# Up products listed ahead of the activation of their bank's other half, and the last quarters listed anew

## The chip, the cores and the metric

The kernel runs on one core of a Trainium2 chip. The metric is device time in microseconds, of the one core. Five engines work side by side, each through its own instruction list in order: TensorE (PE in the profile; its weight loads are PEld), VectorE (DVE), ScalarE (ACT), GpSimd (POOL) and SyncE (SP), which here issues DMAs. An instruction waits, through semaphores, for those of other engines that it depends on.

## The reference

Eight batches of eight heads go through an attention over 32 memory slots; the result, 4608 tokens by 512, goes through two dense layers with a leaky activation between them.

```python
a = softmax(phi over the 32 slots)
k_m, v_m = einsum('bhsm,bhsd->bhmd', a, k), einsum('bhsm,bhsd->bhmd', a, v)
attn = softmax(q @ k_m.T / sqrt(64))
x = attn @ v_m                      # as 4608 x 512
h = x @ w_in                        # 512 x 2048
out = maximum(0.01 * h, h) @ w_out  # 2048 x 512
```

## The kernel before

The value slots of a batch are folded into the first weight matrix (steps `W`), so the up product takes the attention weights themselves. Numbers are split in a high and a low float16 half, and every product is made of three: high by high, high by low, low by high. The order of all work is written out by hand as two strings of step names, `OPENING` and `LATER` (line 67); `run` (line 1447) calls the steps one after the other inside `manual_schedule` (line 1452). Each engine gets its own instructions in that order. Dependencies are drawn from the same order: an instruction waits for the earlier listed ones on other engines that touch what it touches.

The names that matter, with their lines:

- From token 1152 on, the tokens go in groups `G` of 256, each in four quarters `k` of the hidden width (56 quarters; the last group, quarters 52 to 55, has 128 tokens).
- `p{k}.{i}` (`up_late`, line 1215; matmuls at 1229): the up product of part `i` (0 to 3) of quarter `k`. All of them write one PSUM bank, `banks["ph"]`: even `i` its half 0, odd `i` its half 1. A group that spans two batches has two sets of six matmuls.
- `v{k}.{i}` (`leaky_late`, 1245): the activation on ScalarE, out of that half, into the float32 buffer of the quarter. There are two such buffers, taken in turn.
- `s{k}` (`add_g`, 1266, VectorE): sums and differences for a product scheme with seven products in place of eight. `c{k}.{h}` (1270, ScalarE) casts the high half of operand group `h` (0 or 1), `l{k}.{h}` (1274, VectorE) makes the low half.
- `d{k}.{n}` (`down_late`, 1297; `down_tile`, 1331, in the last group): the seven (or four) down products of the quarter. `x{G}.…` (1307 to 1317) combines a group's sums, `z{G}.{t}` (`finish`, 1321) scales one output tile on ScalarE and sends it from SyncE in four DMAs. `end` (`store`, 1170 and 1171) evacuates and sends the last tile; it writes the buffer that `z15.1` sent from.
- `a{b}.…` are the attention's steps of batch `b`: `B20` (664) the exponential, `C10` (698) the slot products on PE, `C3k` (736) scales the key slots on ScalarE, `D10` (772) transposes them on PE, `D11` (785) the value slots, `D2` (344) a small spreading product, `q0` and `q1` (575) eight loads of q each, `Q0` and `Q1` (836) flip q on VectorE, `E1` and `E3` (861) are the scores, `S01` to `S08` the second softmax. `W{b}{j}.p` (1020) folds, `.h` and `.l` split the folded weights.

Of the kernel before, what the change touches and what calls it, by code (L numbers as in the profile page):

```python
# [74 lines left out]
O11.0 o1.m3 P14.0 o2.l1 V14.0 C13 o2.s0 P14.1 L13 o2.m0 O11.1 a2.B10 V14.1 o1.n3 o2.n0 o2.s1 P15.0
a2.B20 C14 o2.m1 O12.0 o2.s2 V15.0 o2.n1 o2.m2 a2.C10 L14 P15.1 o2.s3 a2.B3 O12.1 o2.l2 a2.q0 V15.1
o2.n2 o3.s0 a2.q1 o3.k1 o3.k0 o3.l1 P16.0 P16.1 o3.k2 O13.0 V16.0 C15 o2.m3 o3.s1 O13.1 V16.1 C16
o3.l0 o3.s2 o3.m1 a2.C2 a2.C30 i0.l1 o3.l2 o3.m2 P17.0 L15 o3.m3 o3.n3 O14.0 V17.0 L16 a3.phi P17.1
a2.Q0 a2.C3k V17.1 C17 O14.1 o3.n1 a2.D10 i0.l0 a2.Q1 a2.D3 P18.0 O15.0 V18.0 a2.C31 o3.n2 i0.l2
O15.1 o3.m0 P18.1 a2.E1 a2.E22 a2.E3 a3.kv3 i1.k0 L17 a2.E21 a2.E23 V18.1 i1.l0 P19.0 a2.E20 a2.C4  # L80
i1.k1 Z1.2 a3.kv2 P19.1 a2.D11 a2.S01 C18 Z1.1 a3.kv1 Z1.0 a2.S02 L18 V19.0 O16.0 i1.k2 a2.D2 a2.D4
a3.kv0 a2.S03 i1.l2 O16.1 a2.D5 a2.D6 a2.S04 V19.1 P20.0 C19 O17.0 O17.1 o2.n3 V20.0 L19 P20.1
V20.1 i1.l1 C20 i2.k0 P21.0 W20.p a2.S05 i2.k1 O18.0 W20.h0 V21.0 W20.h1 i2.k2 P21.1 L20 O18.1
W20.l1 V21.1 W20.l0 C21 i2.l0 W21.p a2.S06 P22.0 W21.h1 W21.h0 i2.l1 O19.0 V22.0 o3.n0 i2.l2 W21.l0
i3.k1 P22.1 O19.1 i3.k0 W22.p V22.1 a3.A1 i3.k2 L21 a3.A2 W22.h0 P23.0 W22.h1 O20.0 V23.0 a2.S07
P23.1 a3.A4 O20.1 V23.1 a2.S08 i3.l2 C22 i3.l0 W22.l1 C23 W21.l1 O21.0 i3.l1 L23 p0.0 W23.p v0.0
p0.1 W23.h0 p0.2 L22 a3.A3 W23.h1 a3.B10 O21.1 W22.l0 v0.1 a3.B20 W23.l1 a3.C10 O22.0 os2 a3.B3
v0.2 a3.q0 W23.l0 a4.phi a3.C2 p0.3 a3.C30 a3.q1 O22.1 v0.3 a3.C3k s0 c0.0 a3.C31 l0.0 c0.1 a3.D10
l0.1 p1.0 p1.1 a3.D11 v1.0 O23.0 v1.1 a3.C4 p1.2 a3.D3 v1.2 p1.3 a3.Q0 O23.1 v1.3 p2.0 Z2.0 Z2.1 s1
d0.0 Z2.2 p2.1 v2.0 d0.1 v2.1 a3.D2 a4.A1 a3.D4 c1.0 d0.2 c1.1 p2.2 l1.0 d0.3 v2.2 a3.D5 d0.4 a4.A2  # L90
p2.3 a4.A4 p3.0 a3.Q1 a3.D6 l1.1 d0.5 v2.3 a3.E1 a3.E22 d0.6 a3.E3 c2.0 s2 c2.1 p3.1 a3.E23 v3.0
d1.0 v3.1 a3.E20 d1.1 a3.E21 W30.p l2.0 a3.S01 os3 d1.2 a4.kv3 W30.h0 p3.2 W30.h1 a4.kv1 d1.3 v3.2
a4.kv0 d1.4 W30.l0 d1.5 l2.1 W30.l1 p3.3 a3.S02 W31.p a4.kv2 v3.3 c3.0 d1.6 W31.h0 s3 W31.h1 p4.0
a3.S03 p4.1 v4.0 d2.0 v4.1 c3.1 d2.1 a4.A3 l3.0 d2.2 p4.2 d2.3 v4.2 a3.S04 d2.4 d2.5 a4.B10 a3.S05
p4.3 W31.l1 v4.3 p5.0 l3.1 a3.S06 v5.0 d2.6 a4.B20 d3.0 a3.S07 p5.1 W31.l0 a4.C10 s4 v5.1 a3.S08
d3.1 x3.p a4.q0 c4.0 a4.B3 p5.2 d3.2 c4.1 d3.3 x3.0 v5.2 d3.4 p5.3 l4.0 v5.3 x3.1 c5.0 l4.1 x3.2 s5
d3.5 d3.6 p6.0 x3.3 p6.1 l5.0 v6.0 d4.0 p6.2 a4.q1 v6.1 c5.1 d4.1 d4.2 z3.1 a5.phi d4.3 p6.3 l5.1
v6.2 v6.3 d4.4 a4.C2 a4.C30 d4.5 d4.6 p7.0 p7.1 a4.Q0 d5.0 a4.C3k s6 a4.D10 c6.0 a4.D3 l6.0 v7.0
# [12 lines left out]
p14.1 v14.0 d12.0 a5.q1 p14.2 a5.B3 d12.1 d12.2 l13.1 a5.C2 a5.C30 d12.3 a5.Q0 v14.1 v14.2 d12.4
a6.phi a5.C3k p14.3 d12.5 v14.3 a5.D10 a5.D3 c14.0 d12.6 s14 p15.0 a5.C31 v15.0 l14.0 c14.1 p15.1
d13.0 a5.Q1 l14.1 v15.1 d13.1 z5.1 d13.2 p15.2 d13.3 v15.2 d13.4 d13.5 d13.6 p15.3 p16.0 a5.E1
a5.E22 a5.C4 a5.E3 a6.kv2 a5.E23 a5.E20 d14.0 v15.3 z5.0 c15.0 s15 p16.1 a6.kv3 a5.D11 v16.0 a6.kv0
v16.1 a5.D2 a5.D4 c15.1 d14.1 d14.2 a5.D5 a6.kv1 l15.1 p16.2 d14.3 v16.2 a5.E21 d14.4 p16.3 l15.0
d14.5 v16.3 W42.p c16.0 a6.A1 s16 d14.6 W42.h1 p17.0 W42.h0 W42.l1 a5.S01 a5.D6 p17.1 v17.0 W42.l0
# [12 lines left out]
d22.6 c24.0 p25.0 W52.l1 a6.A3 W52.l0 p25.1 v25.0 a6.B10 l24.0 d23.0 v25.1 d23.1 x8.p c24.1 d23.2
x8.0 p25.2 l24.1 d23.3 v25.2 d23.4 x8.1 p25.3 x8.2 a6.B20 d23.5 v25.3 W53.p c25.0 s25 d23.6 W53.h0  # L130
p26.0 W53.h1 p26.1 x8.3 v26.0 d24.0 W53.l1 z8.1 a6.C10 v26.1 c25.1 a6.q0 d24.1 W53.l0 l25.0 d24.2
p26.2 l25.1 p26.3 v26.2 d24.3 d24.4 d24.5 v26.3 c26.0 s26 c26.1 d24.6 a6.B3 p27.0 p27.1 v27.0 d25.0
p27.2 v27.1 l26.1 a6.q1 a6.C2 d25.1 a6.C30 l26.0 d25.2 a6.C31 p27.3 d25.3 a7.phi v27.2 a6.C3k a6.C4
a6.D10 v27.3 s27 a6.D11 d25.4 a6.Q0 z8.0 d25.5 a6.D3 c27.0 d25.6 c27.1 p28.0 a6.D2 a6.D4 p28.1
v28.0 d26.0 v28.1 a6.D5 l27.1 d26.1 a6.Q1 d26.2 p28.2 d26.3 a6.D6 v28.2 a7.A1 p28.3 p29.0 a6.E1
a6.E22 d26.4 a6.E3 a7.kv3 a6.E20 a6.E23 d26.5 v28.3 a6.E21 W60.p l27.0 c28.0 s28 a7.kv2 d26.6
W60.h0 W60.l0 l28.0 p29.1 a7.kv0 v29.0 a6.S01 d27.0 v29.1 d27.1 x9.p os6 c28.1 d27.2 a7.kv1 W61.p
W60.h1 x9.0 p29.2 l28.1 W61.h0 d27.3 v29.2 W61.h1 d27.4 x9.1 p29.3 x9.2 d27.5 a6.S02 v29.3 d27.6
c29.0 p30.0 x9.3 p30.1 s29 v30.0 d28.0 v30.1 d28.1 l29.0 c29.1 d28.2 p30.2 l29.1 d28.3 v30.2 z9.1
# [1345 lines left out]
```

## Time and profile before

| what | us |
|---|---|
| time, median of 3 runs | 653.35 |
| lowest, highest | 652.09, 653.45 |
| the profiled execution, from first to last instruction | 653.44 |
| ScalarE's up activations of the late part (line 1245), 224 | 99.3 busy, 466 ns each |
| down products of the late part (line 1297), 2184 matmuls | about 287 busy in three groups |
| the last group's down products (1331) | 1% of the chain |

In the profile the engines' busy times stand first, then the chain of work that ended last, followed back from the end: what it names is what the time was spent on. A list of waits says, for each line of an engine, which line of another engine ended its idle time: total, count, longest. In a timeline each row has start, duration, engine, line, operation, operands, count and, in brackets, the idle time before it with what ended it. Rows of like instructions that follow each other are merged into one.

### The profile page before, as it was taken

Reading aid. Unit: us, or ns where it says so; the run is one execution under the profiler, and the core shown is the slowest. Engines: PE = TensorE matmul, PEld = TensorE weight load, DVE = VectorE, ACT = ScalarE, POOL = GpSimd, SP = SyncE. Lnnn points to the kernel's source line nnn. Section 1 sums busy time; section 2 is a strip of 40 time slices with the busy share of each in tenths; the row PEclk is TensorE's granted clock in tenths of the full one; section 3 lists DMA queues with packets and bytes.
Section 4 is the critical chain, followed back from the end, with each engine's and each line's share of the span. In section 5 each row is a group of like instructions: output and inputs, shape, how many; then the busy total and the mean of one; then the engine's idle time right before and its main releaser. Section 6 shows DMA issues by size and latency. Waiting matters only on the chain.

```text
span 653.4 us, 17090 instructions
## 1 busy us (share of the span) xinstructions
PE 635.2 (97%) x7256; PEld 476.3 (73%) x7256; DVE 515.4 (79%) x863; ACT 392.5 (60%) x671; POOL 29.5 (5%) x37
## 2 busy tenths in 40 slices
...
DVE  5675889998996899899969975889887897575641
...
GB/s 237 405 340 332 246 89 85 46 7 104 194 3 25 142 155 56 111 124 35 25 117 158 1 33 43 11 134 146 34 15 80 27 29 22 14 29 6 34 1 50
DMA packets 85309, 61.16 MB, mean 94 GB/s; under 512 B 61936, under 2 KB 68336, under 8 KB 85232
## 3 DMA queue, kind: packets, MB, share of 16 engines
q1 hardware_dynamic: 85136, 59.94, 33.3%
q8 instruction: 57, 0.93, 0.6%
...
## 4 chain that ended last, share of the span: by engine, by line
PE 94%; DMA 2%; ACT 2%; SPq 1%; DVE 0%; issue 0%; ACTq 0%
PE po L1297 31%; PE ph L1229 22%; PE po L1186 16%; PE ph L1114 8%; PE ph L1297 5%; PE pa L1020 4%; PE pa L698 3%; DMA arena<-in_moe_w_in_dram 2%; PE po L1331 1%; PE pa L861 1%; PE pa L1387 1%; ACT wi L1245 1%; PE pa L887 0%; PE pa L344 0%; SPq L549 0%
## 5 line engine op out<-in xcount | busy, mean ns | idle before, releaser
L1297 PEld LDWEIGHTS <-arena 128*128 128x128 f16 x2184 | 209.9, 98 | 31.9 <-issue 8.8
L1245 ACT ACTIVATE wi<-ph,g_sc 128x256 f32<-128x256 f32 (+1 forms) x224 | 99.3, 466 | 164.4 <-PE ph L1229 156.9
L1229 PE MATMUL ph<-a,w_mem 128*128 128x256 f16 (+3 forms) x1440 | 145.3, 246 | 2.9 <-ACT wi L1245 2.9
L1229 PEld LDWEIGHTS <-w_mem 128*128 128x128 f16 x1440 | 114.6, 98 | 17.9 <-issue 6.3
L1297 PE MATMUL po<-arena 128*128 128x256 f16 x936 | 122.2, 273 | 0.0
L1297 PE MATMUL po<-wo,arena 128*128 128x256 f16 x936 | 122.1, 273 | 0.0
L1186 PE MATMUL po<-wo,arena 128*128 128x512 f16 (+1 forms) x384 | 110.3, 433 | 0.0
L1274 DVE TENSOR_TENSOR arena<-arena 128x1024 f16<-128x1024 f32 x52 | 63.6, 1223 | 22.4 <-ACT arena L1270 22.4
L1274 DVE TENSOR_TENSOR arena<-wi,arena 128x768 f16<-128x768 f32 (+1 forms) x60 | 54.7, 912 | 10.1 <-ACT arena L1270 10.1
L1266 DVE TENSOR_TENSOR arena<-wi 128x256 f32<-128x256 f32 x104 | 40.4, 430 | 25.6 <-ACT wi L1245 25.1
L1270 ACT CAST arena<-arena 128x1024 f16<-128x1024 f32 x52 | 54.5, 1047 | 8.2 <-DVE arena L1266 8.0
L1114 PE MATMUL ph<-a,w_mem 128*128 128x192 f16 (+2 forms) x304 | 52.2, 317 | 0.7 <-ACT t L936 0.7
L1186 PEld LDWEIGHTS <-arena 128*128 128x128 f16 x288 | 27.9, 98 | 29.7 <-issue 0.6
L1270 ACT CAST arena<-wi 128x768 f16<-128x768 f32 (+1 forms) x60 | 46.6, 777 | 1.5
L1266 DVE TENSOR_TENSOR arena<-wi,arena 128x256 f32<-128x256 f32 x104 | 45.8, 440 | 1.8
L1297 PE MATMUL ph<-wo,arena 128*128 128x256 f16 x312 | 42.6, 273 | 0.0
L985 POOL TENSOR_TENSOR a<-t,a 128x1024 f16<-128x1024 f32 (+2 forms) x16 | 21.9, 1385 | 431.9 <-ACT a L980 431.9
L1186 PEld LDWEIGHTS po<-wo,arena 128*128 128x128 f32 x96 | 17.7, 190 | 20.3 <-issue 18.5
L1020 PE MATMUL pa<-wi,vT 64*32 64x512 f16 (+1 forms) x704 | 28.9, 420 | 0.4 <-ACT vT L805 0.4
L1114 PEld LDWEIGHTS <-w_mem 128*128 128x128 f16 x240 | 20.7, 98 | 10.3 <-issue 4.1
L1053 ACT ACTIVATE w_mem<-pa 128x512 f16<-128x512 f32 x40 | 22.7, 596 | 8.4 <-PE pa L1020 7.4
L1121 ACT ACTIVATE arena<-ph,g_sc 128x384 f32<-128x384 f32 x32 | 18.4, 581 | 15.6 <-PE ph L1114 15.3
...
## 6 DMA issues: line engine op xcount, KB each, us to landing
out_dram<-obs SPq DMA_DIRECT2D x142, 64.0 KB, 1.7
...
```

The lines of the kernel that those rows point to most:

```text
L698: nc.tensor.matmul(var["pk"][g][hh * M:(hh + 1) * M, cs], ld["phi"][rows, hh, j, :], ld["kv", hh][rows, kinds[0]:kinds[-1] + 1, j, :], sta ...
L985: nc.gpsimd.tensor_tensor(piece(lo, tb), piece(t2, tb), piece(hi, tb), ALU.subtract)
L1020: nc.tensor.matmul(pf[g][cols, :], lhs, rhs, start=(n == 0), stop=(n == len(passes) - 1), tile_position=(g * D, hh * M),)
L1053: nc.scalar.activation(tiles(halves(w16(b, j), g)[:, 0]), w(g), AF.Copy, scale=ws)
L1114: nc.tensor.matmul(ph[:, t0:t0 + n * SB], lhs, rhs, start=(m == 0), stop=(m == len(seq) - 1))
L1186: nc.tensor.matmul(po, lhs, rhs, start=(f == 0 and m == 0), stop=(f == NQ * NF - 1 and m == len(seq) - 1),)
L1229: nc.tensor.matmul(ph[:, t0:t0 + n], lhs, rhs, start=(m == 0), stop=(m == len(seq) - 1))
L1245: nc.scalar.activation(dst, ph, AF.Prelu, scale=g_sc2[:, j:j + 1], alpha=SLOPE)
L1266: nc.vector.tensor_tensor(gt[:, x], y, z, op)
L1270: nc.scalar.copy(dst[:, 0], src)
L1274: nc.vector.tensor_tensor(dst[:, 1], src, dst[:, 0], ALU.subtract)
L1297: nc.tensor.matmul(acc, g[:, x, s, u], rhs, start=(h == 0 and j == 0 and u == 0 and m == 0), stop=(j == NQ - 1 and u == 1 and m == 2), ski ...
```

## The change

Only the string `LATER` changes. It has the same 1834 steps; some thirty stand at another place. No step is added, removed or altered. The string is wrapped at a fixed width, so the diff rewrites many lines; below are its moves, with the neighbours of each, by letters that are used from here on.

```diff
 A
-p1.2 a3.D3 v1.2 p1.3 a3.Q0 O23.1 v1.3 p2.0
+p1.2 p1.3 a3.D3 v1.2 a3.Q0 O23.1 v1.3 p2.0
 B and C
-p4.3 W31.l1 v4.3 p5.0 l3.1 a3.S06 v5.0 d2.6 a4.B20 d3.0 a3.S07 p5.1 W31.l0 a4.C10 s4 v5.1 a3.S08 d3.1 x3.p
+p4.3 W31.l1 p5.0 v4.3 l3.1 a3.S06 v5.0 d2.6 a4.B20 d3.0 a3.S07 p5.1 W31.l0 s4 v5.1 a3.S08 d3.1 a4.C10 x3.p
 D
-v7.3 c7.0 s7 a5.kv0 p8.1 v8.0 v8.1 a4.E20 a5.kv3 c7.1 a4.E21 a4.E23 l7.1 p8.2 a5.kv1 d6.3 a4.D11 v8.2 d6.4
-a4.D2 a4.D4 p8.3 d6.5 a4.S01 l7.0 a4.S02 v8.3 p9.0
+v7.3 v8.0 c7.0 s7 a5.kv0 p8.1 p8.2 v8.1 a4.E20 a5.kv3 c7.1 a4.E21 a4.E23 l7.1 a5.kv1 d6.3 d6.4 p8.3 a4.D11
+v8.2 a4.D2 a4.D4 d6.5 a4.S01 l7.0 a4.S02 v8.3 p9.0
 E
-c8.0 d7.2 c8.1 p9.2 x4.0 d7.3 v9.2 a4.S03 d7.4 x4.1 p9.3
+c8.0 d7.2 p9.2 x4.0 d7.3 v9.2 c8.1 a4.S03 d7.4 x4.1 p9.3
 F
-s14 p15.0 a5.C31 v15.0 l14.0 c14.1 p15.1 d13.0 a5.Q1 l14.1 v15.1 d13.1 z5.1 d13.2 p15.2
+s14 p15.0 p15.1 a5.C31 v15.0 l14.0 c14.1 d13.0 a5.Q1 l14.1 v15.1 d13.1 z5.1 d13.2 p15.2
 G
-p27.3 d25.3 a7.phi v27.2 a6.C3k a6.C4 a6.D10 v27.3 s27 a6.D11 d25.4 a6.Q0 z8.0 d25.5
+p27.3 a6.C3k d25.3 a7.phi v27.2 a6.C4 v27.3 s27 a6.D11 d25.4 a6.D10 a6.Q0 z8.0 d25.5
 H
-p34.1 v34.0 d32.0 l33.0 c33.1 a7.A3 d32.1 d32.2 z10.0 l33.1 p34.2 W63.h0 v34.1 d32.3 v34.2 W63.l0 p34.3 z10.1
-d32.4 W63.l1 a7.B10 d32.5 v34.3 c34.0 s34 p35.0 p35.1 d32.6 a7.B20 v35.0 l34.0 a7.C10
+p34.1 v34.0 v34.1 d32.0 l33.0 c33.1 a7.A3 d32.1 d32.2 z10.0 l33.1 p34.2 W63.h0 d32.3 p34.3 v34.2 W63.l0
+d32.4 W63.l1 a7.B10 d32.5 v34.3 c34.0 s34 p35.0 p35.1 d32.6 a7.B20 z10.1 v35.0 l34.0 a7.C10
 I
-p38.0 x11.3 W70.p s37 v38.0 z11.0 p38.1 d36.0 v38.1 l37.0
+p38.0 x11.3 W70.p p38.1 s37 v38.0 z11.0 d36.0 v38.1 l37.0
 J
-x15.3 v54.0 l53.1 d52.0 z15.0 z15.1 p54.1 d52.1 v54.1 p54.2 c54.0 d52.2 v54.2 l54.0 p54.3 d52.3 v54.3 p55.0
-c54.1 d53.0 l54.1 v55.0 p55.1 d53.1 v55.1 p55.2 c55.0 d53.2 l55.0 v55.2 p55.3 d53.3 v55.3 d54.0 c55.1 l55.1
-d54.1 d54.2 d54.3 d55.0 d55.1 d55.2 d55.3 end
+x15.3 v54.0 l53.1 d52.0 p54.1 v54.1 c54.0 d52.1 p54.2 v54.2 l54.0 d52.2 p54.3 v54.3 c54.1 d52.3 p55.0 v55.0
+l54.1 d53.0 p55.1 v55.1 c55.0 d53.1 p55.2 v55.2 l55.0 z15.0 d53.2 p55.3 v55.3 c55.1 z15.1 d53.3 l55.1 d54.0
+d54.1 d54.2 d54.3 d55.0 d55.1 d55.2 d55.3 end
```

PE's own order differs in three places: in C, where C10 follows d3.1; in D, where d6.4 and p8.3 come ahead of D11 and D2; and in G, where D10 follows d25.4. Everywhere else PE runs the same list, and what differs is which instructions of other engines stand ahead of its own.

More of the change, by code (lines that the diff above doesn't have):

```diff
@@ L75 @@
[L75 to L98, printed above, removed]
@@ L111 @@
[L111 to L116, printed above, removed]
@@ L129 @@
[L129 to L139, printed above, removed]
@@ L146 @@
-c33.1 a7.A3 d32.1 d32.2 z10.0 l33.1 p34.2 W63.h0 v34.1 d32.3 v34.2 W63.l0 p34.3 z10.1 d32.4 W63.l1
-a7.B10 d32.5 v34.3 c34.0 s34 p35.0 p35.1 d32.6 a7.B20 v35.0 l34.0 a7.C10 d33.0 v35.1 c34.1 d33.1
-d33.2 l34.1 p35.2 d33.3 v35.2 a7.B3 d33.4 a7.q0 a7.C2 p35.3 a7.C30 d33.5 v35.3 d33.6 c35.0 s35
-a7.q1 p36.0 p36.1 v36.0 l35.0 d34.0 v36.1 a7.C31 c35.1 a7.C4 d34.1 a7.D11 a7.C3k d34.2 l35.1 p36.2
-a7.Q0 a7.D10 v36.2 d34.3 a7.D3 d34.4 p36.3 a7.D2 v36.3 d34.5 c36.0 d34.6 s36 a7.Q1 p37.0 p37.1
-v37.0 d35.0 v37.1 d35.1 a7.D4 x11.p d35.2 p37.2 a7.D5 x11.0 d35.3 a7.E1 p37.3 c36.1 a7.D6 v37.2
@@ L152 @@
-a7.E22 a7.E3 x11.1 l36.1 os7 d35.4 d35.5 a7.E20 v37.3 d35.6 c37.0 a7.E21 l36.0 x11.2 p38.0 x11.3
-W70.p s37 v38.0 z11.0 p38.1 d36.0 v38.1 l37.0 d36.1 d36.2 z11.1 a7.E23 p38.2 d36.3 v38.2 a7.S01
-W70.h0 d36.4 p38.3 p39.0 W70.l0 c37.1 l37.1 d36.5 a7.S02 W70.h1 d36.6 v38.3 W71.p c38.0 s38 a7.S03
-p39.1 l38.0 v39.0 d37.0 v39.1 a7.S04 c38.1 d37.1 d37.2 W71.h0 p39.2 W71.h1 l38.1 d37.3 v39.2 d37.4
-a7.S05 p39.3 d37.5 W70.l1 v39.3 d37.6 c39.0 s39 p40.0 p40.1 v40.0 l39.0 d38.0 v40.1 a7.S06 c39.1
-d38.1 d38.2 l39.1 p40.2 d38.3 v40.2 W71.l1 a7.S07 d38.4 W71.l0 p40.3 d38.5 a7.S08 v40.3 d38.6 c40.0
@@ L174 @@
-d50.4 p52.3 d50.5 v52.3 d50.6 c52.1 l52.1 p53.0 p53.1 v53.0 d51.0 v53.1 d51.1 x15.p c53.0 d51.2
-l53.0 p53.2 x15.0 d51.3 v53.2 d51.4 x15.1 p53.3 x15.2 d51.5 v53.3 d51.6 c53.1 p54.0 x15.3 v54.0
-l53.1 d52.0 z15.0 z15.1 p54.1 d52.1 v54.1 p54.2 c54.0 d52.2 v54.2 l54.0 p54.3 d52.3 v54.3 p55.0
-c54.1 d53.0 l54.1 v55.0 p55.1 d53.1 v55.1 p55.2 c55.0 d53.2 l55.0 v55.2 p55.3 d53.3 v55.3 d54.0
-c55.1 l55.1 d54.1 d54.2 d54.3 d55.0 d55.1 d55.2 d55.3 end
+a2.A2 W11.l1 V9.0 o1.k0 a2.A4 W11.l0 V9.1 O8.0 W02.h0 o1.l0 W02.h1 C9 o1.k1 O8.1 W02.l1 o1.k2 W02.l0
@@ new lines @@
+o3.s0 a2.q1 o3.k1 o3.k0 o3.l1 P16.0 P16.1 o3.k2 O13.0 V16.0 C15 o2.m3 o3.s1 O13.1 V16.1 C16 o3.l0
+o3.s2 o3.m1 a2.C2 a2.C30 i0.l1 o3.l2 o3.m2 P17.0 L15 o3.m3 o3.n3 O14.0 V17.0 L16 a3.phi P17.1 a2.Q0
+a2.C3k V17.1 C17 O14.1 o3.n1 a2.D10 i0.l0 a2.Q1 a2.D3 P18.0 O15.0 V18.0 a2.C31 o3.n2 i0.l2 O15.1
+o3.m0 P18.1 a2.E1 a2.E22 a2.E3 a3.kv3 i1.k0 L17 a2.E21 a2.E23 V18.1 i1.l0 P19.0 a2.E20 a2.C4 i1.k1
+Z1.2 a3.kv2 P19.1 a2.D11 a2.S01 C18 Z1.1 a3.kv1 Z1.0 a2.S02 L18 V19.0 O16.0 i1.k2 a2.D2 a2.D4 a3.kv0
@@ new lines @@
+W23.l0 a4.phi a3.C2 p0.3 a3.C30 a3.q1 O22.1 v0.3 a3.C3k s0 c0.0 a3.C31 l0.0 c0.1 a3.D10 l0.1 p1.0
+p1.1 a3.D11 v1.0 O23.0 v1.1 a3.C4 p1.2 p1.3 a3.D3 v1.2 a3.Q0 O23.1 v1.3 p2.0 Z2.0 Z2.1 s1 d0.0 Z2.2
+p2.1 v2.0 d0.1 v2.1 a3.D2 a4.A1 a3.D4 c1.0 d0.2 c1.1 p2.2 l1.0 d0.3 v2.2 a3.D5 d0.4 a4.A2 p2.3 a4.A4
+p3.0 a3.Q1 a3.D6 l1.1 d0.5 v2.3 a3.E1 a3.E22 d0.6 a3.E3 c2.0 s2 c2.1 p3.1 a3.E23 v3.0 d1.0 v3.1
+a3.E20 d1.1 a3.E21 W30.p l2.0 a3.S01 os3 d1.2 a4.kv3 W30.h0 p3.2 W30.h1 a4.kv1 d1.3 v3.2 a4.kv0 d1.4
@@ new lines @@
+a4.C2 a4.C30 d4.5 d4.6 p7.0 p7.1 a4.Q0 d5.0 a4.C3k s6 a4.D10 c6.0 a4.D3 l6.0 v7.0 v7.1 a4.Q1 c6.1
+d5.1 a4.C31 d5.2 l6.1 p7.2 d5.3 v7.2 d5.4 a4.C4 a5.A1 d5.5 d5.6 d6.0 p7.3 p8.0 z3.0 d6.1 a4.E1
+a4.E22 d6.2 a4.E3 a5.kv2 v7.3 v8.0 c7.0 s7 a5.kv0 p8.1 p8.2 v8.1 a4.E20 a5.kv3 c7.1 a4.E21 a4.E23
+l7.1 a5.kv1 d6.3 d6.4 p8.3 a4.D11 v8.2 a4.D2 a4.D4 d6.5 a4.S01 l7.0 a4.S02 v8.3 p9.0 a4.D5 W32.p s8
+d6.6 W32.h0 W32.h1 p9.1 W32.l0 v9.0 d7.0 W32.l1 v9.1 d7.1 a4.D6 x4.p os4 c8.0 d7.2 p9.2 x4.0 d7.3
+v9.2 c8.1 a4.S03 d7.4 x4.1 p9.3 l8.0 x4.2 d7.5 v9.3 W33.p c9.0 l8.1 d7.6 W33.h1 p10.0 W33.h0 x4.3
@@ new lines @@
+p13.3 x5.1 a5.C10 x5.2 v13.3 c13.0 s13 d11.5 a5.q0 l13.0 d11.6 c13.1 p14.0 x5.3 p14.1 v14.0 d12.0
+a5.q1 p14.2 a5.B3 d12.1 d12.2 l13.1 a5.C2 a5.C30 d12.3 a5.Q0 v14.1 v14.2 d12.4 a6.phi a5.C3k p14.3
+d12.5 v14.3 a5.D10 a5.D3 c14.0 d12.6 s14 p15.0 p15.1 a5.C31 v15.0 l14.0 c14.1 d13.0 a5.Q1 l14.1
+v15.1 d13.1 z5.1 d13.2 p15.2 d13.3 v15.2 d13.4 d13.5 d13.6 p15.3 p16.0 a5.E1 a5.E22 a5.C4 a5.E3
+a6.kv2 a5.E23 a5.E20 d14.0 v15.3 z5.0 c15.0 s15 p16.1 a6.kv3 a5.D11 v16.0 a6.kv0 v16.1 a5.D2 a5.D4
+c15.1 d14.1 d14.2 a5.D5 a6.kv1 l15.1 p16.2 d14.3 v16.2 a5.E21 d14.4 p16.3 l15.0 d14.5 v16.3 W42.p
```

136 lines of the change are left out of this document (85 added, 51 removed).

## The prediction

> **What bounds the kernel now.** I read the page's busy shares and its chain first, then the list of what TensorE (PE) waited for, then the timeline at each of those waits.
>
> ```profile
> span 653.4 us, 17090 instructions
> ...
> PE 635.2 (97%) x7256; PEld 476.3 (73%) x7256; DVE 515.4 (79%) x863; ACT 392.5 (60%) x671; POOL 29.5 (5%) x37
> ...
> DVE  5675889998996899899969975889887897575641
> ...
> PE 94%; DMA 2%; ACT 2%; SPq 1%; DVE 0%; issue 0%; ACTq 0%
> ...
> out_dram<-obs SPq DMA_DIRECT2D x142, 64.0 KB, 1.7
> ```
> ```profile
> PE ph L1229 <- ACT wi L1245: 3.3, 6, 0.9
> ...
> PE pa L772 <- ACT x_k L736: 0.3, 1, 0.3
> ```
>
> PE is busy for 635.2 of 653.4 us and is 94% of the chain that ended last, so the end moves when PE stalls less, and hardly otherwise. In the late part (from about 200 us on) PE's list holds only these two rows: six waits of up products (line 1229) for an activation (1245), and one of the key transpose (772) for ScalarE's scaling (736). That list counts idle time only; the stall is longer. One six-matmul block is drawn 0.82 us long, yet the next starts 0.65 us after it (246.49 against 245.84 in the second fence below): 0.17 us of a drawn block is the tail that the next one covers. **A stall is thus the idle time shown plus 0.165 us.** The timeline at the last of the seven:
>
> ```profile
> 635.85 0.37 ACT L1245 ACTIVATE wi<-ph,g_sc 128x128 f32<-128x128 f32 x1 [0.84 <-PE ph L1229]
> ...
> 636.24 1.34 ACT L1321 ACTIVATE obs<-obs,osc 128x512 f32<-128x512 f32 x2
> 636.29 0.33 PE L1229 MATMUL ph<-a,arena 128*128 128x128 f16 x3
> ...
> 636.63 0.81 PE L1331 MATMUL po<-wo,arena 128*128 128x512 f16 x3
> ...
> 637.48 0.35 ACT L1245 ACTIVATE wi<-ph,g_sc 128x128 f32<-128x128 f32 x1
> ...
> 637.88 0.33 PE L1229 MATMUL ph<-a,arena 128*128 128x128 f16 x3 [0.44 <-ACT wi L1245]
> ...
> 649.15 0.48 ACT L1170 ACTIVATE obs<-po,osc 128x256 f32<-128x256 f32 x1 [5.02 <-PE po L1331]
> ```
>
> This is p54.2, which writes half 0 of the shared bank. The activation that reads half 0 (v54.0) ended at 636.22, before even d52.1 began; p54.2 started at 637.88, 0.05 us after v54.1 ended, and v54.1 reads the *other* half. So a product waits for every activation listed before it on that bank, whichever half it reads. That is the row on which the whole prediction rests. It also shows why v54.1 was late: the two output scalings (z15.0, z15.1; 1.34 us) stood before it on ScalarE.
>
> **The change part by part.** TensorE's list of steps changes order in three places only (C, D, G below); no instruction is added or removed. All times are on the clock of before, and a stall's end is compared with the earliest start that the new order allows.
>
> A, p1.3 ahead of v1.2:
>
> ```profile
> 217.48 0.47 ACT L1245 ACTIVATE wi<-ph,g_sc 128x256 f32<-128x256 f32 x1 [1.71 <-PE ph L1229]
> 218.01 0.81 PE L1229 MATMUL ph<-a,w_mem 128*128 128x256 f16 x6 [0.56 <-ACT wi L1245]
> ...
> 220.60 0.82 PE L1229 MATMUL ph<-a,w_mem 128*128 128x256 f16 x6
> ```
>
> Stall 0.56 + 0.165 = 0.725. Listed before v1.2, p1.3 follows p1.2 at once, at 217.29, and is drawn to 218.11. Now v1.2 waits for p1.3 instead: it starts at 218.12 in place of 217.48, and the two activations together (0.84 us, the x2 row under D) end at 218.96. The next product on the bank would start at 220.60 − 0.725 = 219.88, so 0.9 us are spare. Worth **0.725**.
>
> B and C, p5.0 ahead of v4.3, and a4.C10 behind d3.1:
>
> ```profile
> 245.84 0.82 PE L1229 MATMUL ph<-a,w_mem 128*128 128x256 f16 x6 [0.56 <-ACT wi L1245]
> ...
> 246.49 0.82 PE L1297 MATMUL po<-arena 128*128 128x256 f16 x6
> ...
> 247.06 1.15 ACT L664 ACTIVATE arena<-arena 128x1152 f32<-128x1152 f32 x1
> ...
> 248.55 2.70 PE L698 MATMUL pa<-arena 64*32 64x128 f32 x144
> ```
>
> The same 0.725. By B p5.0 starts at 245.12 and is drawn to 245.94; v4.3 and v5.0 end at 246.80, and the exponential behind them on ScalarE (line 664, 1.15 us) near 247.9. The slot products C10 (line 698) read its result and would come to 248.55 − 0.725 = 247.82, so about 0.1 would be lost. With d3.1 (0.655) put ahead, C10 starts at 248.48 and waits for nothing; d3.1's operand is made by the cast and lo part of the quarter before, some microseconds earlier. C costs PE nothing; it delays C10's end against PE by 0.655, and with it the q loads that wait for that end. Their flip is placed some 13 us later, so this is hidden; uncovered it would cost those 0.655. Worth **0.725**.
>
> D, v8.0 ahead of c7.0; p8.2 behind p8.1; d6.4 and p8.3 ahead of a4.D11 and a4.D2; and E, c8.1 behind v9.2:
>
> ```profile
> 276.20 0.84 ACT L1245 ACTIVATE wi<-ph,g_sc 128x256 f32<-128x256 f32 x2 [2.21 <-PE ph L1229]
> ...
> 276.93 1.04 ACT L1270 CAST arena<-arena 128x1024 f16<-128x1024 f32 x1
> 277.09 0.33 PE L1229 MATMUL ph<-a,w_mem 128*128 128x64 f16 x6 [0.93 <-ACT wi L1245]
> ...
> 281.64 0.95 DVE L1274 TENSOR_TENSOR arena<-wi,arena 128x768 f16<-128x768 f32 x1
> ...
> 283.66 0.82 PE L1297 MATMUL ph<-wo,arena 128*128 128x256 f16 x6
> ```
>
> Stall 0.93 + 0.165 = 1.10. In the new order p8.2 needs only v8.0, which follows v7.3 on ScalarE long before. p8.2 moves to 275.99 and is drawn to 276.82; v8.1 behind it ends at 277.32, and p8.3, two down blocks later at 277.96, finds it done. The cast c7.1 then ends near 278.26 (before: 277.97), and VectorE's lo part and the chain to d7.0's operand (281.64 to 282.59) stay where they are within 0.2 us, while d7.0 itself moves from 283.66 to 282.57: its spare of 1.07 us is used up to the last tenth. v8.2 and v8.3 follow p8.3 (drawn to 278.80) and end near 279.66, when PE is at 279.62 and wants p9.0: some hundredths lost. Worth **1.09**. E alone frees nothing: c8.1, a cast like c7.1 (1.04 us), would otherwise stand before v9.2, and with PE a microsecond earlier p9.3 would wait about 0.1 us for it.
>
> F, p15.1 ahead of v15.0:
>
> ```profile
> 330.64 1.38 DVE L836 STREAM_TRANSPOSE arena<-arena 128x1152 f32<-128x1152 f32 x1 [1.44 <-DMA arena<-in_q_dram]
> ...
> 332.87 0.82 PE L1229 MATMUL ph<-a,w_mem 128*128 128x256 f16 x6 [0.56 <-ACT wi L1245]
> ...
> 333.49 1.05 ACT L1270 CAST arena<-arena 128x1024 f16<-128x1024 f32 x1 [0.68 <-DVE arena L1266]
> ...
> 334.45 0.47 ACT L1245 ACTIVATE wi<-ph,g_sc 128x256 f32<-128x256 f32 x1
> ...
> 335.48 0.82 PE L1229 MATMUL ph<-a,w_mem 128*128 128x256 f16 x6
> ```
>
> Stall 0.725, but what is late next takes part of it back. VectorE's flip of q (line 836) waited 1.44 us for its loads. Those are issued when C10 ends, so they don't move with this stall. Behind the flip come the additions s14, behind these the cast c14.1 (333.49, released by them), and on ScalarE v15.1 stands behind the cast and ends at 334.92. p15.2 (335.48) could move to 334.76 but waits for v15.1 until 334.97. Worth **0.51**.
>
> G, a6.C3k ahead of v27.2, and a6.D10 behind d25.4:
>
> ```profile
> 432.18 0.17 DVE L726 TENSOR_SCALAR r<-r 128x2 f32<-128x2 f32 x1
> ...
> 433.75 0.51 ACT L736 ACTIVATE x_k<-pa,r 128x64 f32<-128x64 f32 x2
> ...
> 434.31 0.33 PE L772 MATMUL pa<-ident,x_k 128*128 128x128 f32 x1 [0.32 <-ACT x_k L736]
> ```
>
> C3k's factor is ready at 432.35; C3k ran at 433.75 only because v27.2 and p27.3's end stood before it. Listed first it ends near 432.9, and the transpose D10 finds it done. Worth 0.32 + 0.165 = **0.485**.
>
> H, v34.1 and p34.3 moved up, z10.1 down:
>
> ```profile
> 488.72 3.76 SPq L1164 DMA_DIRECT2D out_dram<-obs  x8
> ...
> 490.17 0.82 PE L1229 MATMUL ph<-a,w_mem 128*128 128x256 f16 x6 [0.27 <-ACT wi L1245]
> ...
> 492.27 1.16 ACT L664 ACTIVATE arena<-arena 128x1152 f32<-128x1152 f32 x1
> ...
> 496.37 0.61 SPq L575 DMA_DIRECT2D arena<-in_q_dram  x1
> ```
>
> Worth 0.27 + 0.165 = **0.435**. z10.1 carries four output DMAs of SyncE's in-order queue with it, ahead of the sixteen q loads that go out at 496.37, when C10 has ended. In the new order z10.1 follows the exponential, which ended at 493.43, and ends near 494.0; four sends at 3.76 / 8 = 0.47 us are issued by 495.9, and C10 ends 0.435 earlier than before, at 495.93. They just fit; were they late, the q loads would slip by as much, at most 1.9 us.
>
> I, p38.1 ahead of v38.0:
>
> ```profile
> 520.89 0.72 ACT L1321 ACTIVATE obs<-obs,osc 128x512 f32<-128x512 f32 x1 [0.72 <-DVE obs L1317]
> ...
> 522.99 0.82 PE L1229 MATMUL ph<-a,w_mem 128*128 128x256 f16 x6
> ```
>
> There was no stall, since weight products lie in between. v38.0 now waits for p38.1 and ends near 521.68; z11.0 (0.72) and v38.1 follow and end near 522.65, while p38.2 starts at 522.99. **0**; at most 0.4 lost if something else gets before them.
>
> J, the last quarters: v54.1 no longer stands behind the scalings. p54.1 is drawn from 636.29 through its second part to 636.79, so v54.1 can run from 636.83 to 637.19 and p54.2 start at 637.27. Worth 0.44 + 0.165 = **0.60**. The scalings now come behind v55.2 and c55.1, where nothing on PE waits soon. z15.1 writes and sends the buffer that the final evacuation (649.15, by then 648.54) overwrites: its activation ends near 644.15, its four sends queue behind z15.0's and the last is issued at 646.0; with the page's 1.7 us to landing that is 647.7, 0.8 us ahead.
>
> Sum: 0.725 + 0.725 + 1.09 + 0.51 + 0.485 + 0.435 + 0.60 = 4.57 us, of 4.80 that the seven stalls hold. 653.44 − 4.57 = 648.87. The median of the runs shown is 0.09 below this execution's span, so **648.8 us**.
>
> **The rivals.** *First: the stall moves from inside the pair to behind it.* After two products in one bank both activations must end before the next product: 0.185 + 0.84 + 0.05 = 1.08 us after the second. Where only one 0.655 block lies between, 0.42 is lost again; at all six pairs (A, B, D, F, H, I) that is 2.5 us, of which F's 0.2 is counted already: 648.8 + 2.3 = 651.1 us. For it: F, where it happens in part. Against it: everywhere else two blocks or more (1.31 us) lie between. The Trainium skill (Perfetto Trace Analysis, Matmuls) states the rule behind this rival: independent matmul groups should rotate through different PSUM banks, so that the evacuation of one overlaps the next one's matmuls. By that rule the pairs should gain little; the trace agrees in part, for within one bank p54.2 did wait, at 637.88.
>
> *Second: VectorE sets the pace where it is full.* Its row has five 9s and an 8 in the slices 15 to 20 (about 229 to 327 us), where A's, B's and D's gains arrive. PE then runs into operands that VectorE makes late: d7.0 has 1.07 us to spare. If VectorE held all of B, D and F's part back, 0.725 + 1.09 + 0.51 = 2.3 us return: 651.1 us. Against it: the other down products of that stretch have over 1.5 us, and short gaps in VectorE's stream end in waits for PE, so it follows.
>
> *Third: the pairs' order changes no wait,* since the wait isn't by the listing. Then only G and J count: 653.35 − 1.09 = 652.3 us. The other-half wait of p54.2 speaks against it.
>
> *Fourth, slower: a late activation is carried round.* At six pairs an activation starts about 0.65 us later. If cast, lo part and down product were as tight behind it as p54.2 was behind v54.1, each pair would lose 0.655 instead of gaining, with G and J kept: 653.35 + 6 × 0.655 − 1.09 = 656.2. It decides wherever a down product has less to spare than 0.655 plus the gain so far; d7.0 is the only one near.
>
> **How the numbers follow.** Forecast 0.71, first rival 0.11, second 0.09, third 0.06, fourth 0.03. The forecast's own range is 648.0 to 649.8: no more than all seven stalls and a few tenths for the runs' scatter on one side, D's and H's tight fits on the other. The range given, 647.9 to 651.3, takes in the first two rivals. A measurement of this kernel can tell about 0.2%, 1.3 us: faster has 0.71 + 0.11 + 0.09 = 0.91, the same 0.06 (third rival), slower 0.03.
>
> **What would show it.** Right: PE's list of waits has no late row for line 1245 over 0.3 us in total except at F (0.1 to 0.2 idle), the transpose 772 no row, d7.0 no wait, and the final evacuation starts near 644.6 (649.15 − 4.57). Wrong: waits of line 1229 behind the pairs (first rival), of line 1297 for 1274 between 229 and 327 us (second), unchanged waits (third), or the last evacuation waiting for a DMA.

## The result and the profile after

| | before | after |
|---|---|---|
| time, median of 6 runs, us | 653.47 | 649.52 |
| lowest, highest | 652.09, 653.80 | 647.50, 651.06 |
| the profiled execution, first to last instruction | 653.44 | 647.48 |
| start of p0.0, the late part's first up product | 200.97 | 199.33 |
| start of the final evacuation | 649.15 | 643.20 |
| **the late part between these two** | **448.18** | **443.87** |

The ratio of the times is 0.9942, with a 95% interval of 0.9926 to 0.9958: 3.95 us faster, 2.7 to 4.8 by the interval. The forecast was 648.8, with a range of 647.9 to 651.3: the median lies inside the range, 0.7 us above the forecast.

The two spans differ by 5.96 us, the two times by 3.95. Most of what the spans differ by beyond that is the opening: p0.0 starts 1.64 us earlier in the second profile, though nothing ahead of it was changed. So the change is read from the stretch that both kernels run alike, from p0.0 to the final evacuation: **4.31 us**. All line numbers of the kernel after are lower by one, since its string is one line shorter: the up product is line 1228, its activation 1244, the down product 1296, C10 697, the exponential 663.

The page of the kernel after (span and busy times; VectorE's row of fortieths; the chain's shares):

```profile
span 647.5 us, 17093 instructions
...
PE 634.2 (98%) x7256; PEld 476.6 (74%) x7256; DVE 515.1 (80%) x863; ACT 391.3 (60%) x671; POOL 29.5 (5%) x37
...
DVE  5775889998996899899969975789977897575641
...
PE 94%; DMA 2%; SPq 1%; ACT 1%; DVE 1%; issue 0%; DVEq 0%; ACTq 0%
...
L1228 PE MATMUL ph<-a,w_mem 128*128 128x256 f16 (+3 forms) x1440 | 144.8, 246 | 0.2 <-ACT wi L1244 0.2
```

TensorE's share of the chain is as before. The last row is the up products' group: 0.2 us of idle time ahead of them. Its list of waits in the late part:

```profile
core 0 of [0], span 647.5 us
engine line waited for: us in total, times, longest us
...
PE ph L1228 <- ACT wi L1244: 0.2, 1, 0.2
```

Six waits of 3.3 us became one of 0.2 us, and the key transpose has no row any more. The last quarters now, beside the rows of 635 to 638 us of before (start, duration, engine, line, operands; in brackets idle time and what ended it):

```profile
630.24 0.81 PE L1330 MATMUL po<-wo,arena 128*128 128x512 f16 x3
630.44 0.37 ACT L1244 ACTIVATE wi<-ph,g_sc 128x128 f32<-128x128 f32 x1 [0.84 <-PE ph L1228]
...
630.89 0.33 PE L1228 MATMUL ph<-a,arena 128*128 128x128 f16 x3
...
636.34 0.37 ACT L1244 ACTIVATE wi<-ph,g_sc 128x128 f32<-128x128 f32 x1 [0.18 <-PE ph L1228]
...
636.61 0.71 ACT L1320 ACTIVATE obs<-obs,osc 128x512 f32<-128x512 f32 x1
636.79 0.50 PE L1228 MATMUL ph<-a,w_mem 128*128 128x128 f16 x6
...
637.32 0.37 ACT L1244 ACTIVATE wi<-ph,g_sc 128x128 f32<-128x128 f32 x1
...
638.15 0.72 ACT L1320 ACTIVATE obs<-obs,osc 128x512 f32<-128x512 f32 x1
```

The first three rows are d52.1, v54.1 and p54.2, the product that waited 0.44 us before: v54.1 now runs while d52.1 does, and p54.2 follows d52.1 without a wait. Further down the output scalings (1320) stand alone, each behind an activation (1244) that was wanted sooner, and no row of line 1228 carries a wait.

Site by site, from the starts of two TensorE steps that enclose each (us, after minus before):

| stretch | site | forecast | measured |
|---|---|---|---|
| p1.2 to p2.0 | A | −0.725 | −0.72 |
| p4.3 to p5.1 | B | −0.725 | −0.72 |
| p5.1 to p5.2 | C10 of batch 4 | 0 | −0.29 |
| p7.3 to p9.1 | D, E | −1.09 | −1.06 |
| p14.3 to p15.3 | F | −0.51 | −0.37 |
| p27.1 to p28.0 | G | −0.485 | −0.54 |
| p34.1 to p35.1 | H | −0.435 | −0.43 |
| p35.1 to p36.0 | C10 of batch 7 | 0 | +0.35 |
| p53.3 to d55.3 | J | −0.60 | −0.60 |

All the stretches between these agree within 0.03 us, and the one from d55.3 to the final evacuation within 0.05: a gain made at one site stays a gain until the end, except where a row above takes it back.

### The profile page after: what moved, and what is told of

The parts are those of the page before. It is cut to its first block, busy times and chain, and to the rows that moved or that the text cites. A ratio compares the mean times of both kernels' runs of the same rounds, so it can differ in the third digit from the quotient of the medians.

```text
span 647.5 us, 17093 instructions
## 1 busy us (share of the span) xinstructions
PE 634.2 (98%) x7256; PEld 476.6 (74%) x7256; DVE 515.1 (80%) x863; ACT 391.3 (60%) x671; POOL 29.5 (5%) x37
## 4 chain that ended last, share of the span: by engine, by line
PE 94%; DMA 2%; SPq 1%; ACT 1%; DVE 1%; issue 0%; DVEq 0%; ACTq 0%
PE po L1296 31%; PE ph L1228 22%; PE po L1185 16%; PE ph L1113 8%; PE ph L1296 5%; PE pa L1019 4%; PE pa L697 3%; DMA arena<-in_moe_w_in_dram 2%; PE po L1330 2%; PE pa L860 1%; SPq L574 1%; PE pa L1386 1%; DMA arena<-in_q_dram 0%; PE pa L886 0%; PE pa L343 0%
```

## The experiments

"Late part" is the stretch from p0.0 to the final evacuation, in us. For a kernel with a single run, it is compared in place of the time, since the opening alone moves by 4 us from profile to profile (last section). Single pauses of TensorE, of 0.1 to 0.7 us, the longer ones credited to "issue", come and go between profiles as well; the kernel after, profiled a second time, took 444.15 us, with such a pause of 0.53 us behind C10 of batch 7 and 0.21 us less at F.

**1. The pairs undone.** Sites A, B, D, F, H and I as before; C, E, G and J stay.

```diff
-p1.2 p1.3 a3.D3 v1.2
+p1.2 a3.D3 v1.2 p1.3
-p5.0 v4.3 l3.1
+v4.3 p5.0 l3.1
...
-s14 p15.0 p15.1 a5.C31 v15.0
+s14 p15.0 a5.C31 v15.0 l14.0 c14.1 p15.1
...
```

> The changed kernel with the moves A, B, D, F, H and I taken back; C, E, G and J stay. Measured by the late part, from the start of p0.0 to the start of the last evacuation: 448.18 us before, 443.82 after. Theory (a product waits for every activation listed ahead of it on its bank): the stalls return where they were, 0.72 at p1.3, 0.72 at p5.0, 1.1 at p8.2, 0.72 at p15.1 and 0.44 at p34.3; net of what F and H lost again elsewhere the late part is 446.6 to 447.2. Rival (the pairs' order changes no wait, and the gain came from G, J and the opening): it stays at 443.8 within 0.3.

Late part 446.80 (time 650.5, kernel before beside it 652.37). Its list of TensorE's waits:

```profile
PE ph L1228 <- ACT wi L1244: 2.9, 5, 0.9
```

Five of the six are back, with TensorE's starts showing losses of 0.726, 0.726, 1.09, 0.726 and 0.437 us at p1.3, p5.0, p8.2, p15.1 and p34.3; the sixth of before, p54.2, stays away with J. The order on ScalarE and TensorE alone makes and removes these waits. The difference to the kernel after, 2.93 us, is less than the 3.49 forecast for these sites, mostly by what F and the C10 of batch 7 had given back; a pause of 0.27 us at d3.4 and shorter C10 of batches 4 and 5 nearly cancel.

**2. C10 of batch 4 back ahead of d3.1.**

```diff
-p5.1 W31.l0 s4 v5.1 a3.S08 d3.1 a4.C10
+p5.1 W31.l0 a4.C10 s4 v5.1 a3.S08 d3.1
```

> The changed kernel with move C taken back: C10 of batch 4 ahead of d3.1 again. As the prediction had it, C10 meets the exponential about 0.1 us too early: the late part grows from 443.82 by 0.1 to 0.2. Rival, formed from the two traces: C10's 144 matmuls cannot all be issued before about 2.95 us after the exponential B20 has ended, whenever PE comes to them (2.63 us long with 0.33 us to spare, 2.35 with 0.62, 2.21 with 0.76); then C10 still ends near 2.97 us after B20's end, d3.1 comes on top, and the late part grows by 0.6 to 0.7.

The slot products of this kernel and of the kernel after (exponential, C10):

```profile
246.08 1.16 ACT L663 ACTIVATE arena<-arena 128x1152 f32<-128x1152 f32 x1
...
247.29 2.98 PE L697 MATMUL pa<-arena 64*32 64x128 f32 x144
```
```profile
244.34 1.16 ACT L663 ACTIVATE arena<-arena 128x1152 f32<-128x1152 f32 x1
...
246.13 2.42 PE L697 MATMUL pa<-arena 64*32 64x128 f32 x144
```

C10 waited only 0.09 us, yet from its start to the next product it took 2.91 us in place of 2.35. p5.2 came 0.68 us later, not 0.1 as the prediction priced it. 0.28 us of it were regained at p15.2, which has no row in the list of waits here, so the late part was 444.21, 0.34 more than after. Here, and in the kernels before and after wherever C10 begins less than 0.8 us behind its exponential, it ends 2.96 to 3.05 us after the exponential's end, however early TensorE got there. That is what the rival had said, and it became a second theory: **work whose operand was released shortly before costs TensorE time that no wait shows.**

**3. C10 of batches 4, 5 and 7 one block later.**

```diff
-d3.1 a4.C10 x3.p a4.q0 c4.0 a4.B3 p5.2
+d3.1 x3.p a4.q0 c4.0 a4.B3 p5.2 a4.C10
-x5.1 a5.C10 x5.2 v13.3 c13.0 s13 d11.5
+x5.1 x5.2 v13.3 c13.0 s13 d11.5 a5.C10
-l34.0 a7.C10 d33.0
+l34.0 d33.0 a7.C10
```

Here the q loads of batch 4 stand ahead of its C10, so its slot products read q in place of what they should.

> The changed kernel with C10 of the batches 4, 5 and 7 each listed one block later (behind p5.2, d11.5 and d33.0); no other step moves. Issue theory: the blocks fill the time in which C10's instructions are issued, so C10 shrinks from 2.35, 2.72 and 2.57 us to 2.2 each, and the late part from 443.82 to 442.6 to 443.0. Rival (C10's length is set by its operands or by chance): lengths scatter as before, late part 443.8 within 0.2.

All three took 2.18 us, where the kernel after has 2.35, 2.72 and 2.57: the second theory's length. The late part was nevertheless 445.18, above both forecasts, because batch 4's move had been drawn up badly: behind d3.1, p5.2 lost 1.48 us waiting for its activation, d3.4 came 0.66 late, and p15.2 lost 0.62. The lengths of batches 5 and 7 count; batch 4's C10 read another operand, and the sum doesn't count.

**4. v15.1 directly behind v15.0.**

```diff
-v15.0 l14.0 c14.1 d13.0 a5.Q1 l14.1 v15.1
+v15.0 v15.1 l14.0 c14.1 d13.0 a5.Q1 l14.1
```

> The changed kernel with v15.1 listed directly behind v15.0, ahead of the cast c14.1. Theory of F (p15.2 waits because v15.1 stands behind the cast, which waits for s14 behind the flip of q, which waits for its loads): the 0.35 us that p15.2 loses in the changed kernel vanish, late part 443.4 to 443.5. Rival (the activations of a pair are late by themselves): the stall stays at 0.3 or more.

Late part 443.61; p15.2 waits no more and comes 0.35 us sooner. The 0.1 us by which the forecast was missed is mostly a pause of 0.08 at d3.4. F's rest was v15.1 behind the cast c14.1, as the prediction had it. The chain in the kernel after (flip of q, its wait for the loads, the cast, v15.1, p15.2):

```profile
326.39 1.38 DVE L835 STREAM_TRANSPOSE arena<-arena 128x1152 f32<-128x1152 f32 x1 [1.59 <-DMA arena<-in_q_dram]
...
329.24 1.05 ACT L1269 CAST arena<-arena 128x1024 f16<-128x1024 f32 x1 [0.17 <-DVE arena L1265]
...
330.20 0.47 ACT L1244 ACTIVATE wi<-ph,g_sc 128x256 f32<-128x256 f32 x1
...
330.71 0.49 PE L1228 MATMUL ph<-a,w_mem 128*128 128x256 f16 x3 [0.19 <-ACT wi L1244]
```

**5. The last quarters alone, in the kernel before.**

```diff
-d52.0 z15.0 z15.1 p54.1
+d52.0 p54.1
-l55.0 v55.2 p55.3 d53.3 v55.3 d54.0 c55.1 l55.1
+l55.0 z15.0 v55.2 p55.3 d53.3 v55.3 d54.0 c55.1 z15.1 l55.1
```

> The kernel before with part J alone: z15.0 behind l55.0 and z15.1 behind c55.1. If the prediction's term stands, p54.2 starts behind d53.1 with no wait (0.60 us), nothing else moves, and from p0.0 to the final evacuation it takes 448.18 - 0.60 = 447.58 us (447.5 to 447.7). If the 0.60 was given to the last quarters only because the parts ahead of them had shifted ScalarE, the wait of 0.44 us stays and it is 448.2. If the final evacuation is held by the sends of z15.1, a wait for a DMA stands before it.

Late part 447.86. The wait of p54.2 is gone (0.60), but 0.30 us are lost at p55.3. It starts 0.95 us after the down product ahead of it, where 0.65 is usual; the list of waits has no row for it, since the drawn end of that product covers most of the wait:

```profile
642.01 0.72 ACT L1320 ACTIVATE obs<-obs,osc 128x512 f32<-128x512 f32 x1
...
642.08 0.81 PE L1330 MATMUL po<-wo,arena 128*128 128x512 f16 x3
...
642.63 0.35 ACT L1244 ACTIVATE wi<-ph,g_sc 128x128 f32<-128x128 f32 x1
...
643.03 0.49 PE L1228 MATMUL ph<-a,w_mem 128*128 128x128 f16 x6
```

The activation shown is v55.2, and p55.3 starts 0.05 us after its end. Here z15.0 stands ahead of v55.2; in the kernel after it stands behind it, since J also moved the activations ahead of the down products. So J's two halves belong together: the scalings moved alone keep half of the 0.60.

**6. A pair with one block behind it.**

```diff
-p20.0 l19.0 p20.1 v20.0 z6.1 d18.0 v20.1 c19.1 d18.1 d18.2 l19.1 z6.0 p20.2
+p20.0 l19.0 p20.1 v20.0 z6.1 d18.0 v20.1 p20.2 c19.1 d18.1 d18.2 l19.1 z6.0
```

> The kernel after with p20.2 moved ahead by a block, so that only d18.0 (0.655 us) lies between the pair p20.0, p20.1 and the next product in the same bank. The prediction's first rival priced this place: both activations need 0.185 + 0.84 + 0.05 = 1.08 us after the second product, so p20.2 would wait and 0.42 us would be lost: 443.87 + 0.42 = 444.29 us from p0.0 to the final evacuation (444.2 to 444.4), with a late row of line 1228 for 1244 of 0.2 to 0.3 us at that product. If activations of a pair cost nothing beyond the block that covers them, it stays at 443.87.

```profile
369.32 0.82 PE L1296 MATMUL ph<-wo,arena 128*128 128x256 f16 x6
369.52 0.47 ACT L1244 ACTIVATE wi<-ph,g_sc 128x256 f32<-128x256 f32 x1 [1.45 <-PE ph L1228]
...
369.89 0.71 ACT L1320 ACTIVATE obs<-obs,osc 128x512 f32<-128x512 f32 x1
370.50 0.46 ACT L1244 ACTIVATE wi<-ph,g_sc 128x256 f32<-128x256 f32 x1
...
371.02 0.82 PE L1228 MATMUL ph<-a,w_mem 128*128 128x256 f16 x6 [0.88 <-ACT wi L1244]
```

p20.2 lost 1.04 us, not 0.42, and the late part was 445.20; the rest of the excess over 444.29 is pauses at d3.4 and p15.2 (0.20 and 0.10 more than in the kernel after). The mechanism is the first rival's. My price had left out z6.1, an output scaling listed between v20.0 and v20.1: its 0.61 us from start to start is the difference. This is what the forecast escaped at the six pairs, where at least two blocks' time follows (1.3 us; at F the cast stood between the two activations, and p15.2 waited even so).

**7. The exponential of batch 5 earlier, TensorE's order untouched.**

```diff
-v13.2 a5.B20 d11.4 p13.3
+a5.B20 v13.2 d11.4 p13.3
```

> The kernel after with one step moved on ScalarE alone: the exponential of batch 5 (a5.B20) ahead of v13.2, which was waiting 0.57 us for TensorE. TensorE's order is untouched, and C10 of batch 5 starts at the same point behind p13.3. Its operand is then ready about 1.4 us before it, in place of 0.33. Theory (work released only just before it is wanted costs issue time that no wait shows): C10 falls from 2.72 to 2.18 us, and from p0.0 to the final evacuation it takes 443.87 - 0.54 = 443.33 us. Rival (C10's 2.72 us is set by where it stands among TensorE's blocks or by its data's place): it stays at 2.72 and the sum at 443.87.

**8. The same with d11.5 ahead of p13.3.**

```diff
-a5.B20 v13.2 d11.4 p13.3 x5.1 a5.C10 x5.2 v13.3 c13.0 s13 d11.5
+a5.B20 v13.2 d11.4 d11.5 p13.3 x5.1 a5.C10 x5.2 v13.3 c13.0 s13
```

> The kernel a5_b20 with one block put ahead: d11.5 before p13.3, so that TensorE's order is d11.4, d11.5, p13.3, C10. In a5_b20 C10 of batch 5 took 2.384 us although its operand was ready 1.37 us before; my reading is that p13.3 just ahead of it had itself been released (by v13.2, ending at 315.97) only 0.24 us before it began, so that the sequencer was late on both. With one more block ahead, v13.2 ends about 0.9 us before p13.3 begins: then C10 takes 2.18 us. If it is the up product as its neighbour, or the batch's data, that makes C10 longer, it stays near 2.38. From p0.0 to the final evacuation about 443.2 us by the first, 443.4 by the second.

First of run 7, then of run 8: activation v13.2, the product p13.3 that it releases, C10 and the next down block.

```profile
315.48 0.48 ACT L1244 ACTIVATE wi<-ph,g_sc 128x256 f32<-128x256 f32 x1
...
316.21 0.82 PE L1228 MATMUL ph<-a,w_mem 128*128 128x256 f16 x6
...
316.96 2.45 PE L697 MATMUL pa<-arena 64*32 64x128 f32 x144
...
319.35 0.83 PE L1296 MATMUL po<-wo,arena 128*128 128x256 f16 x6
```
```profile
312.23 0.48 ACT L1244 ACTIVATE wi<-ph,g_sc 128x256 f32<-128x256 f32 x1
...
313.62 0.82 PE L1228 MATMUL ph<-a,w_mem 128*128 128x256 f16 x6
...
314.37 2.25 PE L697 MATMUL pa<-arena 64*32 64x128 f32 x144
...
316.55 0.72 PE L1296 MATMUL po<-wo,arena 128*128 128x256 f16 x5
```

Run 7 moved only ScalarE's list, and C10 fell from 2.72 to 2.38 us: neither its place among the blocks nor its data alone sets its length. It did not fall to 2.18, though its operand lay ready for 1.37 us; but the product just ahead had been released only 0.24 us before it began. In run 8 that product was released 0.91 us ahead, and C10 took 2.18. The late part was 443.37 in run 7, near the 443.33 expected, but by luck: C10 gave 0.34 us of the 0.54, and p15.2 gave 0.28, for the flip came 7.64 us after C10's end, against 8.05 in the kernel after. In run 8 it was 444.55, far above both forecasts. With d11.5 moved ahead, one block (0.655 us) fewer lies between C10 and p15.2, and the q loads and the flip behind C10 took 8.56 us: p15.2 waited 1.35 us of idle time, and came 1.16 later against the rest than in the kernel after, which is these 0.655 and 0.51 together. **What is taken out of the stretch between C10 and p15.2 is given back as far as p15.2 hangs on those loads.**

**9 to 11. Two kernels with these moves together, and the kernel after again beside the first of them.**

```diff
 best, against the kernel after
-a3.B10 O21.1 W22.l0 v0.1 a3.B20
+a3.B10 O21.1 W22.l0 a3.B20 v0.1
-p5.0 v4.3 l3.1 a3.S06 v5.0 d2.6 a4.B20
+p5.0 a4.B20 v4.3 l3.1 a3.S06 v5.0 d2.6
-v13.2 a5.B20
+a5.B20 v13.2
-v15.0 l14.0 c14.1 d13.0 a5.Q1 l14.1 v15.1
+v15.0 v15.1 l14.0 c14.1 d13.0 a5.Q1 l14.1
-a7.C10 d33.0
+d33.0 a7.C10
...
 best2, against best
-a5.B20 v13.2 d11.4 p13.3 x5.1 a5.C10 x5.2 v13.3 c13.0 s13 d11.5
+v13.2 a5.B20 d11.4 p13.3 x5.1 x5.2 v13.3 c13.0 s13 d11.5 a5.C10
...
```

The lines left out are small blocks put next to their neighbours: d4.1, d12.1, d22.4 and d25.1, of which best2 leaves d25.1 where it was.

> The kernel after with what the runs so far would save: v15.1 directly behind v15.0 (0.26), the exponentials of batches 3, 4 and 5 listed earlier on ScalarE (a3.B20 ahead of v0.1: 0.48; a4.B20 ahead of v4.3: 0.17; a5.B20 ahead of v13.2: 0.54), a7.C10 one block later (0.385), and four small blocks d4.1, d12.1, d22.4, d25.1 directly behind their neighbours (0.07 each at most, 0.1 taken). By the theory of released work it takes 443.87 - 1.94 = 441.9 us from p0.0 to the final evacuation, and the time falls from 649.5 to 647.6 us; without that theory only 0.36 us are gained: 649.2.

> The kernel named best with two steps mended: d25.1 stays where it was (its move had brought the transpose D11 of batch 6 up to VectorE's chain, 0.42 us lost), and C10 of batch 5 stands behind d11.5 with its exponential where it was, in place of the earlier exponential (2.18 us for C10 in place of 2.31). From p0.0 to the final evacuation 442.58 - 0.42 - 0.13 = 442.0 us (441.8 to 442.4, since single blocks of TensorE have shown pauses of 0.1 to 0.5 us in some runs); its time 647.8 us.

> The kernel after once more, unaltered, beside the kernel named best on the same chip: from p0.0 to the final evacuation 443.87 us within 0.1, its time 649.5 with the scatter of the first 190 us (1.5 us each way), so that the two kernels can be compared by their medians and by that stretch.

| kernel | median of 6 runs | ratio to before, 95% interval | late part |
|---|---|---|---|
| after, first | 649.52 | 0.9942 [0.9926, 0.9958] | 443.87 |
| after, again | 649.06 | 0.9931 [0.9913, 0.9948] | 444.15 |
| best | 648.34 | 0.9918 [0.9902, 0.9935] | 442.58 |
| best2 | 648.10 | 0.9917 [0.9894, 0.9940] | 442.58 |

Both take 1.3 to 1.6 us out of the late part, where 1.9 had been expected. In best, the move of d25.1 cost 0.42 us: it had stood between a6.C2 and D11, and without it D11 waited for VectorE's chain. In best2 a pause of 0.68 us fell on d33.2, shortly behind batch 7's C10:

```profile
490.84 0.60 PE L1296 MATMUL po<-arena 128*128 128x256 f16 x4
...
491.95 0.38 PE L1296 MATMUL po<-arena 128*128 128x256 f16 x2 [0.52 <-issue]
```

No instruction of another engine is named for it (0.53 us at the same block in the second profile of the kernel after, 0.13 in best, none in the first). The times follow by their medians. best, run beside the kernel after on one chip, is 0.7 us below it; best2 ran on another chip, beside the kernel before alone. The intervals of all four ratios overlap: that the two are faster than the kernel after rests on the late part, from one profile each of best and best2, not on the times.

From the profiles of all kernels, C10 (144 small products; its length is from its first start to the start of the next block) against the time for which its operand lay ready:

| kernel, batch | ready ahead, us | length, us |
|---|---|---|
| run 2, batch 4 | 0.05 | 2.91 |
| before, 4 | 0.33 | 2.63 |
| before, 5 | 0.33 | 2.72 |
| after, 7 | 0.40 | 2.57 |
| after, 4 | 0.62 | 2.35 |
| before, 7 | 0.76 | 2.21 |
| run 1, 4 | 0.98 | 2.18 |
| best2, 4 | 3.45 | 2.18 |
| after, 6 | 4.53 | 2.18 |
| run 7, 5 (product ahead released 0.24 us before) | 1.37 | 2.38 |
| run 8, 5 | 2.02 | 2.18 |

## Why the prediction was right, point by point

**The wait goes by the bank: right.** The six waits that the prediction traced to an activation of the bank's other half went, at five sites with that activation listed later and at J with it ahead of the scalings, and the five whose old order run 1 restored came back. Only F left a smaller one behind. The Trainium skill (PSUM — Partial Sum Buffer, PSUM bank collisions raise a hardware error) states the rule that such a program keeps: guard this memory by bank and quarter of the partitions, not by address. The trace agrees: a product into half 0 waited 0.44 us of idle time for a reading of half 1. While both halves stay in one bank, order is what can be changed, and the change does that; another bank for one half was not tried.

**A, B, J: right to a hundredth.** 0.72, 0.72 and 0.60. The idle time plus 0.165 us was the right size of a stall. I cost nothing, as forecast: v38.1 ended at 517.28, p38.2 began at 517.59. E was not tried by itself.

**C: right that it costs nothing, wrong what it is worth.** The step "about 0.1 would be lost" without it failed: run 2 lost 0.68. And C10 of batch 4 became 0.29 shorter by B and C together, for its operand was ready 0.62 us ahead in place of 0.33.

**D: right.** 1.06 of 1.09, with d7.0's spare shrunk from 1.07 to 0.18 us: its operand was done at 279.09, it began at 279.27. "Used up to the last tenth" was slightly too dark.

**F: mechanism right, size off.** v15.1 behind the cast did hold p15.2 (run 4), for 0.35 us in place of the 0.21 of the working. The term that was mis-sized is the assumption that the flip stands still against C10: it came 8.05 us after C10's end, 7.91 before, and 7.5 to 8.6 over all profiles, because the q loads land at varying times (the eighth 7.3 to 8.4 us after that end).

**G: right**, 0.54 for 0.485.

**H: the stall went (0.43), and nearly all of it came back.** The prediction asked whether z10.1's four sends would be late for the q loads; they were not. What it did not ask was whether C10 itself costs more when TensorE reaches it sooner after its exponential. It did: ready 0.40 us ahead in place of 0.76, it took 0.35 us more. H's net is 0.08.

**The sum.** 4.57 forecast, 4.31 found in the late part: H −0.35 and F −0.14 against C10 of batch 4 +0.29, and hundredths. The time came out 3.95 lower by its medians. **The working's anchor was wrong, though:** it took the span of the profiled execution for its time ("0.09 below this execution's span"). In every run with both numbers but one (2.5), the time is 1.9 to 2.0 us above the span (after: 649.41 with a span of 647.48). By that the profiled execution of before took about 655.4, an estimate, with an opening at the late end: its p0.0 starts at 200.97. That the error stayed small is luck: the forecast subtracted from a number that happened to lie near the median: 653.47 − 4.31 is 649.2, and 649.52 was measured. For the final evacuation, forecast near 644.6, the clock of before has to be kept: it lies 443.87 us behind p0.0, the forecast 443.63.

**The rivals.** The first didn't occur at the six pairs beyond F's part; run 6 shows that it holds with one block between, and that anything listed between the two activations adds to it. The second didn't: VectorE's row is as full as before, and d7.0 had room left. The third fell with run 1, the fourth found no down product that waited.
